# An attention-and-gate block on one core: keys in column tiles, norms on GpSimd, loads by use, level maxima

## The chip, the cores and the metric

The kernel runs on one core of a Trainium2 chip. The metric is the time of one execution on the device in microseconds (us). The core has TensorE (PE; its weight loads are shown apart as PEld), VectorE (DVE), ScalarE (ACT), GpSimd (POOL) and SyncE (SP), which here issues nearly all transfers.

## What is computed

x is 2048 rows of 512. It is normalised by rows; from the result come a 32-head attention with one shared key and value head of 16 columns, and a two-layer network with Mish between (1792 hidden). The output is x + attention * silu(network):

```python
xn = _layernorm(x, axis=-1)
q = (xn @ wq).reshape(B, S, 32, 16).transpose(0, 2, 1, 3)
k, v = xn @ wk, xn @ wv
p = softmax(einsum("bhqd,bkd->bhqk", q, k) * 16 ** -0.5)
s = einsum("bhqk,bkd->bhqd", p, v).transpose(0, 2, 1, 3).reshape(B, S, 512) @ wo
h = xn @ w1 + b1
g = silu((h * tanh(softplus(h))) @ w2)
return x + s * g
```

## The kernel before, in words

The program is written out by a Python planner: which instruction follows which on an engine is fixed when the program is built; on the chip each engine takes its own list in order and waits for semaphores.

**Blocks.** Rows are taken in four blocks of 512 (C). The attention runs in 32 units (NU), each of four heads of one block: unit v is block v // 8. A unit takes 16 steps of 128 keys, 512 steps (NS) in all.

**A step of the main loop** (the loop at L1483 with waves at L637) has on TensorE: four score products e (e_one, L1028; keys by queries on 64 rows), four products m for a *later* unit's row maxima (m_one, L1048; queries by keys, on 64 or 48 rows), and, for step s - 2, the value products pv (L1113, four column tiles of 32). ScalarE takes the exponentials of e, VectorE the maximum of each m (L1064). The maxima lead by LEAD = 20 steps. The array is used as two halves of 64 rows: one half's matmuls run beside the other's. e of a step stand on one half (a = 1 - s % 2); a chunk of dense-layer products (xps) is cut in half by rows (Mm.half), and runs on the one half in one step and on the other in the next, so each chunk takes two steps.

**Which maxima stand where.** em (L1490) calls m_sides (L1072) with the half of the e: n of the step's maxima go to that half, among the e (EM), the rest to the half of the dense products, where waves issues them behind the last of these. tot is 4, or 5 and then 3 for an odd chunk; MLAG = 4 bounds how far one side may lead; m_next counts the maxima issued of each side.

**Dense work.** Groups of products wait in queue and qqueue: queries (12 products), first layer m1 (12), second layer m2 in thirds of 5, 5 and 4 hidden tiles (15, 15 and 12 products) for four row tiles, and the output projection wo (12). begin (L501) takes the next that is ready, chunk_size (L634) cuts it into equal chunks of at most XMAX = 8: 12 as 6 + 6, 15 as 8 + 7. Weights come by load (L456) in the order of the tags (wq, ws, wb, wx) through two raw buffers and are split by split (L414) into a high and a low part; later blocks load the stored split.

**The lead-in** is planned as tasks with assumed durations, priorities and earliest times (L1382 to L1470): for each block statistics (stats, on VectorE, block 3's on ScalarE), norms (norm_a, norm_b, norm_c), scaling of x (x_scale), transposes (x_transpose), copies (x_copy), then keys and values in one product of 128 columns (k_proj, L315): wkf holds the key weights seven times (columns 0 to 47 and 64 to 111 are used for ks) and the value weights at the end. k_high (ScalarE) and k_low (VectorE) write high and low parts of the keys in place into ks; v_copy, v_transpose and v_out make the values. Query rows reach their places in qt by SP transfers (dmas, L723: twelve for each of the first two units). Between these stand the first maxima, 40 for each side, in pairs; after 34 of each side c_rows (L1082) reduces the first unit's and moves them by eight transfers, and the main loop starts when they land.

Of the kernel before, what the change touches and what calls it, by code (L numbers as in the profile page):

```python
# [80 lines left out]
class Item:  # L81
    def __init__(self, tag, key, src):
        self.tag, self.key, self.src = tag, key, src
        self.raw = self.tile = None
        self.step = None
        self.users = 0


class Group:
# [35 lines left out]
def block_kernel(ctx: ExitStack, tc: tile.TileContext, x, wq, wk, wv, wo, w1, b1, w2, out):  # L125
# [127 lines left out]
    def norm_a(z):  # L253
        if z.start >= A_LO:
            dve.tensor_scalar(ve[:, z], mvs[:, z, 1], 1.0 / D, EPS, op0=ALU.mult, op1=ALU.add)
        else:
            dve.tensor_scalar(ve[:, z], mvs[:, z, 1], EPS, None, op0=ALU.add)
# [5 lines left out]
    def norm_c(z):  # L263
        r, h = rstd[:, z], hv[:, z]
        stt(h, ve[:, z], -0.5, r, ALU.mult, ALU.mult)
        mul(dve, h, h, r)
        stt(r, h, 1.5, r, ALU.add, ALU.mult)
        if z.start >= A_LO:
            mul(dve, nbias[:, z], nbias[:, z], r)
        else:  # L270
            stt(nbias[:, z], mvs[:, z, 0], -1.0, r, ALU.mult, ALU.mult)
# [43 lines left out]
    def k_proj(c, dts):  # L315
        if 0 in dts:
            kp_of[c] = ps_v.tile([P, C], F32, tag="v", name=f"kp{c}")
        for dt in dts:
            pe.matmul(kp_of[c], wkf[:, dt], xf_of[c][dt // 2][:, dt % 2], start=(dt == 0), stop=(dt == 3))  # L319

    KR = slice(0, 112)

    def k_high(c):
        act.activation(ks[KR, C * c:C * (c + 1)], kp_of[c][KR], AF.Identity, bias=kone[KR])

    def k_low(c):
        k = ks[KR, C * c:C * (c + 1)]
        stt(k, f(k), ksgn[KR, 0:1], kp_of[c][KR], ALU.mult, ALU.add)
        kready[c] = now[0] + 0.85

    def v_copy(c):
        vt_of[c] = sb.tile([P, C], F32, tag=f"y{(2, 3, 1, 2)[c]}", name=f"vt{c}", bufs=1)[0:32]
        act.activation(vt_of[c], kp_of[c][96:128], AF.Copy)

    def v_transpose(c):
        vp = vp_of[c] = ps_v.tile([P, 4, 32], F32, tag="v", name=f"vp{c}")
        for tt in range(4):
            pe.transpose(vp[:, tt], vt_of[c][:, P * tt:P * (tt + 1)], ident[0:32, 0:32])

    def v_out(c):  # L340
        dve.tensor_copy(vaug[:, 4 * c:4 * c + 4, 0:DH], vp_of[c][:, :, 16:32])
# [139 lines left out]

    def pump():
        for tag in items:
            while arrived(tag):
                split(tag)
            load(tag)
# [9 lines left out]
    def prepare():  # L496
        for n in range(min(2 if step[0] < NS - LEAD else 8, len(queue))):
            if queue[n].pre and queue[n].pre():
                queue[n].pre = None

    def begin():  # L501
        prepare()
        if qqueue and is_ready(qqueue[0]):
            g = qqueue.popleft()
        elif queue and is_ready(queue[0]):
            g = queue.popleft()
        else:
# [12 lines left out]
        return True  # L520
# [35 lines left out]
    def next_group(z):  # L556

        if cur["g"] is not None:
            lanes[z] = [cur["g"], cur["n"], cur["ps"], None]
            cur["g"] = None  # L560
            return
# [72 lines left out]
    def chunk_size(n):  # L634
        return -(-n // -(-n // XMAX)) if n else 0

    def waves(h, em, new):  # L637
# [6 lines left out]
        else:  # L644
            g = cur["g"]
            mms = cur["chunk"] or g.mms[cur["n"]:cur["n"] + chunk_size(len(g.mms) - cur["n"])]
# [57 lines left out]
    def q_group(c, b):  # L704
        it = item("wq", ("q", b), wq[:, P * b:P * (b + 1)].rearrange("(t p) n -> p t n", p=P))

        def post(ps):
# [12 lines left out]
            for k in range(2):  # L720
                v = 8 * c + 2 * b + k

                def dmas(v=v, k=k, parts=((0, 0), (0, 1), (1, 0), (1, 1))):  # L723
                    q = qt_of[v] = qts[v % 3]
                    for p, a in parts:
                        o = 64 * a
                        r = 64 * k + 16 * (2 * p + a)
                        for d, src in ((o, qh), (o + 16, qh), (o + 32, ql)):
                            sp_at(0.63)
                            sp.dma_start(f(q[d:d + 16, p]), f(src[r:r + 16]))  # L730
                if first:
                    lead["qdma"](lambda ps, dmas=dmas: dmas(parts=[(p, a) for p in ps for a in range(2)]))
# [286 lines left out]
    queue.extend(wo_groups(NC - 1))  # L1019

# [51 lines left out]
    def m_sides(h, k, second):  # L1072
# [6 lines left out]
        n = max(min((k + tot - 4) // 2 if k % 2 else k // 2, hi), lo)  # L1079
# [143 lines left out]

    def when(t):
# [3 lines left out]
        if k <= step[0] and busy[0] + E0 < t + 0.5 and not plan["POOL"]:  # L1228
# [16 lines left out]
    def put_off(g, ps):  # L1245
# [4 lines left out]
        t = task("ACT", 0.69, fn, at=now[0] + lead.get("late", 0.35))  # L1250
# [4 lines left out]
    def q_low(fn):  # L1255
        lead["qlow"] = task("DVE", 0.69, fn, at=T["ACT"] + 0.7)

    def q_dma(fn):
# [3 lines left out]
        def move(p):  # L1262
            fn(ps=(p,))
            qready[v] = (qready[v] or ()) + (now[0] + 6 * 0.63 + 2.0,)
        for p in range(2):
            task("SP", 6 * 0.63, lambda p=p: move(p), [lead["qlow"]], prio=1 + p + 2 * v)
# [25 lines left out]
    st = [task("DVE", 0.83, lambda t=t: stats(t), at=max(xat[t], 15.5 if t > 3 else 0), prio=(0, 1.6, 2.2, 2.8)[t // 4]) for t in range(A_LO)]  # L1292
# [5 lines left out]
    for c0, c1 in ((0, 1), (1, 2), (2, 3), (3, 4)):  # L1298
        z = slice(4 * c0, 4 * c1)
        na = task("DVE", 0.2, lambda z=z: norm_a(z), st[z], prio=c0 and 1)  # L1300
        nb = task("ACT", 0.45, lambda z=z: norm_b(z), [na])
        nrm = task("DVE", 0.8, lambda z=z: norm_c(z), [nb], prio=2 * c0 and 1)
        for c in range(c0, c1):
            xs, scs = [], []
            for t in range(4 * c, 4 * c + 4):
                sc = task(*(("ACT", 0.72), ("DVE", 0.4))[c == 0 and t % 2], lambda t=t: x_scale(t), [nrm])
# [28 lines left out]
            else:  # L1335
# [3 lines left out]
                task("SP", 1.0, keep_x, xs)  # L1339
# [3 lines left out]
            kus = 0.9  # L1343
# [4 lines left out]
            kh = task("ACT", 0.59, lambda c=c: k_high(c), [kp])  # L1348
            kl = task("DVE", 0.68, lambda c=c: k_low(c), [kh])

            vc = task("ACT", 0.59, lambda c=c: v_copy(c), [kp])
# [33 lines left out]
    while True:  # L1385
# [25 lines left out]
        for tag in items:  # L1411
            load(tag)
# [31 lines left out]
        elif k == "J":  # L1444
            tag = next((g for g in ("wq", "ws", "wb") if (g == "wq" or s > 19.0) and arrived(g) and busy[0] + E0 < s + 0.5), None)
# [4 lines left out]
            else:  # L1450
                gap[0] = 0
                if not plan["POOL"]:
# [111 lines left out]
```

## Time and profile before

| | |
|---|---|
| median of 3 runs | 1581.02 us (1580.65 to 1581.16) |
| the profiled execution | 1580.51 us, its span 1578.7 us |
| granted clock of TensorE | 1.00 |
| busy, PE / DVE / ACT / POOL | 99 / 85 / 83 / 40% of the span |
| first score product e | 78.5 us after the span's start |
| DMA | 124.31 MB, mean 79 GB/s |

In rows of the profile, a group or a line of the timeline names the source line, the engine, the operation, the tile written and the tiles read, and their shapes; "x8" is a count of merged instructions. Lines of the timeline begin with the start and the duration in us; in groups the numbers are busy us, mean ns of one, and the engine's idle time before them with what released it. A window line gives start:end, its length, then busy time (and count) of PE, PEld, DVE, ACT and POOL, the granted clock, the share of the DMA engines and GB/s. SPq is SP's queue. A busy TensorE is not TensorE at its peak.

### The profile page before, as it was taken

The page shows a single profiled execution, that of the slowest core. Times are in us where ns is not written, and L with a number is a line of the kernel's source. Part 1 is how long each engine was busy: PE and PEld are TensorE (multiplying, and loading weights), DVE is VectorE, ACT ScalarE, POOL GpSimd, SP SyncE. Part 2 cuts the span into 40 slices and gives each one's busy share as a digit, 9 for nine tenths or more (in the row PEclk, how much of TensorE's full clock was granted, in tenths as well). Part 3 has the DMA queues.
Part 4 walks back from the last instruction along what each step waited for, and adds up shares of the span by engine and source line. Part 5 has one row for each costly group of instructions (what it writes and reads, how often), then busy time and mean ns, then how long its engine had stood idle before and what let it go on. Part 6 is the DMA issues. An engine that isn't in the chain of part 4 may idle for free.

```text
span 1578.7 us, 31652 instructions
## 1 busy us (share of the span) xinstructions
PE 1566.1 (99%) x11717; PEld 842.6 (53%) x11717; DVE 1341.9 (85%) x2341; ACT 1306.6 (83%) x2515; POOL 626.4 (40%) x641
## 2 busy tenths in 40 slices
PE   9999999999999999999999999999999999999998
PEld 5455555555555555555555555555555555555554
DVE  8998888889889888888898988888889998888832
ACT  7488798798998778978988787897898878789886
POOL 3476266274474104613525131362252414225412
PEclk9999999999999999999999999999999999999999
DMA  6233221132321304222122312220332213032011
GB/s 195 94 117 112 65 100 43 55 125 84 124 91 47 103 15 151 58 71 67 39 79 71 109 61 62 81 71 16 124 98 85 69 54 102 18 111 58 15 58 51
DMA packets 74666, 124.31 MB, mean 79 GB/s; under 512 B 21520, under 2 KB 35344, under 8 KB 74512
## 3 DMA queue, kind: packets, MB, share of 16 engines
q1 hardware_dynamic: 74512, 122.29, 25.1%
q8 instruction: 93, 1.52, 0.4%
q14 instruction: 61, 0.50, 0.1%
HBM read 74.78 MB, written 26.21 MB: 64 GB/s over the span
## 4 chain that ended last, share of the span: by engine, by line
PE 96%; DVE 2%; ACT 1%; DMA 0%; SPq 0%; issue 0%; POOL 0%; ACTq 0%; DVEq 0%
PE xps L118 44%; PE pv L1122 32%; PE e L1039 8%; PE m L1060 8%; DVE mb L1064 2%; PE kp L319 1%; PE xps L114 0%; ACT pt L1041 0%; PE xp L287 0%; PE late L118 0%; DMA xin<-in_dram 0%; PE late L1039 0%; PE wop L114 0%; DVE xt L162 0%; SPq L224 0%
## 5 line engine op out<-in xcount | busy, mean ns | idle before, releaser
L1064 DVE TENSOR_REDUCE mb<-m 128x1 f32<-128x512 f32 x2048 | 1274.0, 683 | 175.0 <-PE m L1060 153.4
L1041 ACT ACTIVATE pt<-e 128x512 f32<-128x512 f32 x2018 | 1061.9, 603 | 219.3 <-PE e L1039 210.6
L1060 PE MATMUL m<-ks,qt 48*128 48x512 f32 (+1 forms) x2048 | 830.5, 421 | 1.7 <-DVE mb L1064 0.8
L1039 PE MATMUL e<-qt,ks 64*128 64x512 f32 x2018 | 741.2, 401 | 0.5 <-ACT pt L1041 0.3
L1122 PE MATMUL pv<-pt,vaug 128*32 128x512 f32 x4096 | 543.0, 604 | 0.0
L1060 PEld LDWEIGHTS m<-ks,qt 48*128 48x128 f32 (+1 forms) x2048 | 372.5, 185 | 63.0 <-DVE mb L1064 25.3
L1039 PEld LDWEIGHTS e<-qt,ks 64*128 64x128 f32 x2018 | 373.3, 186 | 18.5 <-ACT pt L1041 6.7
L118 PE MATMUL xps<-wbs,act 64*128 64x512 f32 x1248 | 338.1, 407 | 0.1
L118 PEld LDWEIGHTS xps<-wbs,act 64*128 64x128 f32 x1248 | 217.6, 185 | 172.2 <-ACT pt L1041 100.7
L118 PE MATMUL xps<-xt,ws 64*128 64x512 f32 x1104 | 306.0, 410 | 0.1
L118 PEld LDWEIGHTS xps<-xt,ws 64*128 64x128 f32 x1104 | 190.2, 185 | 183.2 <-ACT pt L1041 116.5
L172 POOL TENSOR_SCALAR t<-t 128x512 f32<-128x512 f32 x56 | 34.4, 614 | 329.3 <-ACT t L784 328.9
L1122 PEld LDWEIGHTS pv<-pt,vaug 128*32 128x32 f32 x4096 | 81.9, 108 | 136.9 <-issue 128.8
L162 POOL TENSOR_TENSOR hb<-hb,t 128x512 f32<-128x512 f32 x56 | 72.3, 1290 | 64.2 <-ACT t L797 44.1
L118 PE MATMUL xps<-xt,wq 64*128 64x512 f32 x336 | 93.2, 410 | 0.0
L118 PEld LDWEIGHTS xps<-xt,wq 64*128 64x128 f32 x336 | 57.9, 185 | 55.5 <-ACT pt L1041 35.2
L118 PE MATMUL xps<-wbs,ot_all 64*128 64x512 f32 x288 | 79.5, 408 | 0.0
L118 PEld LDWEIGHTS xps<-wbs,ot_all 64*128 64x128 f32 x288 | 49.5, 184 | 46.4 <-ACT pt L1041 30.2
L162 POOL TENSOR_TENSOR hb<-hb,u 128x512 f32<-128x512 f32 x56 | 72.3, 1291 | 4.4
L162 POOL TENSOR_TENSOR u<-u,t 128x512 f32<-128x512 f32 x56 | 71.8, 1282 | 4.7
L162 POOL TENSOR_TENSOR act<-hb,act 128x512 fp32r<-128x512 f32 x55 | 70.8, 1287 | 4.6
L162 POOL TENSOR_TENSOR oc<-oc,sc 128x512 f32<-128x512 f32 (+1 forms) x16 | 20.6, 1288 | 116.5 <-ACT sc L1150 72.0
(146 smaller groups left out, 945.6 us busy)
## 6 DMA issues: line engine op xcount, KB each, us to landing
wbs<-w SPq DMA_DIRECT2D x36, 512.0 KB
ws<-w SPq DMA_DIRECT2D x35, 512.0 KB
qt<-qh SPq DMA_DIRECT2D x256, 32.0 KB
wq<-wq SPq DMA_DIRECT2D x14, 512.0 KB
w<-wbs SPq DMA_DIRECT2D x14, 512.0 KB
wbs<-wo SPq DMA_DIRECT2D x12, 512.0 KB
rawws<-in_dram SPq DMA_DIRECT2D x21, 256.0 KB
rawwb<-in_dram SPq DMA_DIRECT2D x20, 256.0 KB
```

The source lines that it names most:

```text
L118: i = self.pe.matmul(ps, self.lhs()[o], self.rhs()[o], start=(self.k == 0 and self.halves == 0), stop=(self.k == self.tot - 1 and self.hal ...
L162: eng.tensor_tensor(out=o, in0=a, in1=b, op=op)
L172: pool.tensor_scalar(o, o, lim, 0.0, op0=ALU.min, op1=ALU.max)
L319: pe.matmul(kp_of[c], wkf[:, dt], xf_of[c][dt // 2][:, dt % 2], start=(dt == 0), stop=(dt == 3))
L1039: pe.matmul(e, ks[o:o + 64, P * k:P * (k + 1)], q[o:o + 64, p], start=True, stop=True)
L1041: r = act.activation(pt, e, AF.Exp, scale=0.25)
L1060: pe.matmul(m, q[o, p, P * t:P * (t + 1)], ks[o, C * kb:C * (kb + 1)], start=True, stop=True)
L1064: r = dve.reduce_max(out=mb_of[v][:, kb, z:z + 1], in_=m, axis=AX.X)
L1122: pe.matmul(o[32 * j:32 * j + 32], vaug[:, k], pt, start=(k == 0), stop=(k == 15))
```

## The change

Keys and values of blocks 1 to 3 are projected with 64 columns of weights in two column tiles, each for half of the block's rows (256), so that the product stands as 128 partitions by 256. High and low parts are made there, in vt, and four transfers for a block place them in ks (k_rows); values are transposed from the same layout. Norms of blocks 1 to 3 and their scaling of x go to GpSimd. The statistics of blocks 2 and 3 are planned from 19.6 us. The first unit's first query rows go partly by ScalarE's queue. Loads are taken in the order in which groups use them. A group of 15 products may be cut in fives (most) when there are steps to spare before the first output projection. m_sides moves one maximum to the other half when the sides are not level. Some waits of the planner for GpSimd look only at tasks that are due.

```diff
+        self.most = XMAX
...
     def norm_c(z):
-        r, h = rstd[:, z], hv[:, z]
+        r, h, b = rstd[:, z], hv[:, z], nbias[:, z]
+        if z.start:
+            charge(1.1)
+            pool.tensor_tensor(out=h, in0=ve[:, z], in1=r, op=ALU.mult)
+            pool.tensor_tensor(out=h, in0=h, in1=r, op=ALU.mult)
+            pool.tensor_scalar(h, h, -0.5, 1.5, op0=ALU.mult, op1=ALU.add)
+            pool.tensor_tensor(out=r, in0=h, in1=r, op=ALU.mult)
+            if z.start < A_LO:
+                pool.tensor_scalar(b, mvs[:, z, 0], -1.0, 0.0, op0=ALU.mult, op1=ALU.add)
+            pool.tensor_tensor(out=b, in0=b, in1=r, op=ALU.mult)
+            return
...
     def x_scale(t):
         x_ = xin[divmod(t, 4)]
-        if t < 4 and t % 2:
+        if t > 3:
+            charge(0.7)
+            pool.tensor_scalar(x_, x_, rstd[:, t:t + 1], nbias[:, t:t + 1], op0=ALU.mult, op1=ALU.add)
+        elif t % 2:
...
+            for h in range(2):
+                pe.matmul(kp_of[c][HALF * h:HALF * (h + 1), 0:KW], wkf[:, dt, HALF:P], x_[:, KW * h:KW * (h + 1)],
+                          start=(dt == 0), stop=(dt == 3))
...
     def k_low(c):
+        if c:
+            st = vt_of[c][:, KW:C]
+            stt(st.bitcast(F32R), st, ksgn[:, 0:1], kp_of[c][:, 0:KW], ALU.mult, ALU.add)
+            return
...
+    def k_rows(c):
+        for a in range(2):
+            for h in range(2):
+                z = C * c + KW * h
+                sp.dma_start(f(ks[HALF * a:HALF * a + 48, z:z + KW]), vt_of[c][HALF * h:HALF * h + 48, KW:C])
+        kready[c] = now[0] + 4 * 0.63 + 2.1
...
+    def by_use():
+        return sorted(items, key=lambda g: items[g][todo[g][1]].use if todo[g][1] < len(items[g]) else 10 ** 6)
+
+    def load_next():
+        order = [g for g in by_use() if todo[g][1] < len(items[g])]
+        for tag in order:
+            for g in order:
+                it, n = items[g][todo[g][1]] if todo[g][1] < len(items[g]) else None, todo[g][1]
+                if g != tag and it and it.use + 3 < items[tag][todo[tag][1]].use and not kept.get(it.key) and (
+                        before(g, n) is None or not before(g, n).users):
+                    break
+            else:
+                load(tag)
...
+    def spare_steps():
+
+        n = next((n for n, g in enumerate(queue) if g.wo is not None), None)
+        if n is None or queue[n].wo:
+            return 0
+        due = 16 * 8 * (queue[n].wo + 1) + 9
+        return due - step[0] - 11 - 4 * (1 + n + sum(32 * (16 - k) - LEAD - 20 < due for k in range(1, len(qqueue) + 1)))
...
+        if len(g.mms) == 15 and spare_steps() > 1:
+            g.most = 5
...
-    def chunk_size(n):
-        return -(-n // -(-n // XMAX)) if n else 0
+    def chunk_size(n, most):
+        return -(-n // -(-n // most)) if n else 0
...
+    for n, g in enumerate(queue):
+        for i in g.items:
+            i.use = i.use or n
+    for n, i in enumerate(items["wq"]):
+        i.use = 8 * n - 7
...
-        n = max(min((k + tot - 4) // 2 if k % 2 else k // 2, hi), lo)
+        n = (k + tot - 4) // 2 if k % 2 else k // 2
+        off = ahead + 2 * n - tot - 2 * h
+        if k and abs(off) > 1:
+            n -= 1 if off > 0 else -1
+        n = max(min(n, hi), lo)
         return n, tot - n
...
+        if not v:
+            fn(parts=[(0, 1)], which=(0, 1), eng=act)
         for p in range(2):
-            task("SP", 6 * 0.63, lambda p=p: move(p), [lead["qlow"]], prio=1 + p + 2 * v)
+            n = 6 if v or p else 3
+            task("SP", n * 0.63, lambda p=p, n=n: move(p, n), [lead["qlow"]], prio=1 + p + 2 * v)
...
-    st = [task("DVE", 0.83, lambda t=t: stats(t), at=max(xat[t], 15.5 if t > 3 else 0), prio=(0, 1.6, 2.2, 2.8)[t // 4]) for t in range(A_LO)]
+    st = [task("DVE", 0.83, lambda t=t: stats(t), at=max(xat[t], (0, 15.5, 19.6, 19.6)[t // 4]), prio=(0, 1.6, 2.2, 2.8)[t // 4]) for t in range(A_LO)]
...
+            if c:
+                kr = task("SP", 4 * 0.63, lambda c=c: k_rows(c), [kl], prio=-4)
+                task("SP", 1.0, keep_x, [kr, *xs])
```

More of the change, by code (lines that the diff above doesn't have):

```diff
@@ L1222, in block_kernel, with pool_due @@
     now = [0.0]
+    def pool_due():
+        return any(all(d.end is not None for d in k.deps) for k in plan["POOL"])
     def when(t):
@@ L1227, in when @@
         k = min(timed, default=1)
-        if k <= step[0] and busy[0] + E0 < t + 0.5 and not plan["POOL"]:
+        if k <= step[0] and busy[0] + E0 < t + 0.5 and not pool_due():
             timed[k].pop(0)()
@@ L1249, in fn @@
             g.done = step[0]
-        t = task("ACT", 0.69, fn, at=now[0] + lead.get("late", 0.35))
+        t = task("ACT", 1.95 if "late" in lead else 0.69, fn, at=now[0] + lead.get("late", 0.35))
         waiting.append(t)
@@ L1255, in q_low @@
     def q_low(fn):
-        lead["qlow"] = task("DVE", 0.69, fn, at=T["ACT"] + 0.7)
+        lead["qlow"] = task("DVE", 0.69, fn, at=T["ACT"] + 0.7, prio=-4)
     def q_dma(fn):
```

82 lines of the change are left out of this document (52 added, 30 removed).

## The prediction

> **What bounds the kernel now.** I read the busy shares and the chain of waits on the page first, then four stretches, then single steps of the main loop on TensorE.
>
> ```profile
> PE 1566.1 (99%) x11717; PEld 842.6 (53%) x11717; DVE 1341.9 (85%) x2341; ACT 1306.6 (83%) x2515; POOL 626.4 (40%) x641
> ...
> PE 96%; DVE 2%; ACT 1%; DMA 0%; SPq 0%; issue 0%; POOL 0%; ACTq 0%; DVEq 0%
> ```
>
> ```profile
> 0.00:78.50 78.50, 73.71 (x292) 41.28 (x294) 70.54 (x148) 48.45 (x107) 34.45 (x44) 1.00 0.48 146
> 78.50:1506.00 1427.50, 1425.69 (x10942) 764.82 (x10940) 1253.96 (x2125) 1204.23 (x2303) 579.94 (x586) 1.00 0.25 76
> ```
>
> TensorE is busy throughout, but in the first 78.5 us part of that is warming and waiting for VectorE; the clock is 1.00 in both stretches. The lead-in is 5% of the span. The other 1427.5 us are some 490 equal steps, so an edit that touches each step's order weighs more than one in the lead-in. Two neighbouring steps, from one pv burst to the next:
>
> ```profile
> 1455.37 1.06 PE L1122 MATMUL pv<-pt,vaug 128*32 128x512 f32 x8
> ...
> 1457.87 0.39 PE L1060 MATMUL m<-ks,qt 48*128 48x512 f32 x1
> 1457.88 0.42 PE L1039 MATMUL e<-qt,ks 64*128 64x512 f32 x1
> 1458.23 1.07 PE L1122 MATMUL pv<-pt,vaug 128*32 128x512 f32 x8
> ...
> 1460.96 0.40 PE L1039 MATMUL e<-qt,ks 64*128 64x512 f32 x1
> 1460.97 0.40 PE L118 MATMUL xps<-wbs,act 64*128 64x512 f32 x1
> 1461.29 1.07 PE L1122 MATMUL pv<-pt,vaug 128*32 128x512 f32 x8
> ```
>
> The first carries six half products (xps), four e and four m: 14 half-array matmuls, seven to each row half, so seven slots; it lasts 1458.23 - 1455.37 = 2.86. The second carries eight, four and four: 16, eight to each half, and lasts 3.06. So a step's length is the count of slots of the **fuller row half**, and one more slot costs 0.2. A step whose halves are uneven stands in this trace too:
>
> ```profile
> 535.34 1.06 PE L1122 MATMUL pv<-pt,vaug 128*32 128x512 f32 x8
> ...
> 538.05 1.06 PE L1122 MATMUL pv<-pt,vaug 128*32 128x512 f32 x8
> 539.04 0.50 PE L118 MATMUL xps<-wbs,act 64*128 64x512 f32 x1
> 539.05 0.49 PE L1060 MATMUL m<-ks,qt 48*128 48x512 f32 x1
> ...
> 539.62 0.39 PE L1060 MATMUL m<-ks,qt 48*128 48x512 f32 x1
> ...
> 540.55 0.63 PE L118 MATMUL xps<-wbs,act 64*128 64x512 f32 x2
> 541.02 0.63 PE L1060 MATMUL m<-ks,qt 48*128 48x512 f32 x2
> 541.58 0.64 PE L1122 MATMUL pv<-pt,vaug 128*32 128x512 f32 x4
> ```
>
> It has the same eight xps, four e and four m, but only two m run beside the products and two run behind them on the products' own half: ten slots against six. It lasts 541.58 - 538.05 = 3.53, which is 0.47 more than the even step: 0.235 for each m left over. The step before it (535.34 to 538.05) has no product and lasts 2.71.
>
> **The levelled maxima.** This is the part that decides. m_sides gives n of a step's maxima to the half that holds the four e, and the rest to the half that holds the products. For eight products the old rule takes n = 4 of 4: sides 8 and 8. The new rule computes off = ahead + 2n - tot - 2h and takes one from n when off is above 1. The count of maxima done is equal on both sides when the loop begins (the lead-in issues them in pairs), call the lead of side 0 over side 1 A = 0. A chunk starts on an even step, with h = 1: off = 0 + 8 - 4 - 2 = 2, so n = 3 and A becomes -2. The next step has h = 0: off = -2 + 8 - 4 = 2, so n = 3 again and A returns to 0. Both steps of every eight-product chunk now have 4 + 3 = 7 matmuls on one half and 8 + 1 = 9 on the other: one slot more. With six products off is 0 in both steps (n = 3, seven and seven as before). With seven, off is 1 and then 0, nothing changes either. A can only be even where a chunk starts, since a pair of steps always takes eight maxima, and for an even A the eight-product chunk is never left alone: from A = 2 or -2 one of its steps is trimmed, and A is 0 after it. An odd start (after one empty step) gives the same with A = -2. So the rule makes this one chunk uneven for good.
>
> How many such steps there are follows from one row of the main loop's groups (line, operation, shapes, count):
>
> ```profile
> L118 PE MATMUL xps<-wbs,act 64*128 64x512 f32 x1218 | 329.9, 407 | 0.1
> ```
>
> These are the halves of the second dense layer. Twelve groups of 12 products (last third, three blocks) make 12 x 24 = 288; the remaining 930 are 31 groups of 15, which are cut 8 + 7, and each eight takes two steps: 62 steps. The limit of five (g.most) takes some away: spare_steps counts 126 - s - 4(1 + groups ahead of the first output projection + q groups due). At the first such group, s is about 16 with 22 groups and 4 q groups ahead: 126 - 16 - 108 = 2, just above 1; the next sees 0. It returns 0 for every later block. So about one group (none to three) is cut 5 + 5 + 5, and 60 (56 to 62) steps stay. 60 x 0.235 = **+14.1** (56 x 0.20 = 11.2 to 62 x 0.24 = 14.9). No other engine hides it: in the main stretch VectorE is busy 1254 and ScalarE 1204 of 1427.5 us.
>
> The group cut in fives gains about 0.8: four steps of 8, 8, 8 and 7 slots, 3 x 3.06 + 2.86 = 12.0, become three pairs of 7 and 6 slots, 3 x (2.86 + 2.71) = 16.7 with the empty step as the floor, and two of these six stood empty before (5.4). And the uneven step at 538 loses one of its two extra slots, 0.24: together **-1.0** (0 to -3). Loading in order of use may remove the empty steps (some three, 2.7 each), but what they take up is worth only its slots.
>
> **The lead-in.** From the first maximum to the last one needed (68 of 80) VectorE sets the pace; the window and its groups, shortened to those touched:
>
> ```profile
> 24.40:72.70 48.30, 47.09 (x185) 23.44 (x183) 46.06 (x83) 30.72 (x70) 19.89 (x19) 1.00 0.36 115
> ```
>
> ```profile
> L1064 DVE TENSOR_REDUCE mb<-m 128x1 f32<-128x512 f32 x68 | 42.2, 683 | 2.7 <-PE m L1060 2.4
> L237 DVE SCALAR_TENSOR_TENSOR ks<-ks,ksgn,kp 112x512 fp32r<-112x512 f32 x3 | 2.2, 736 | 0.0
> L237 DVE SCALAR_TENSOR_TENSOR hv<-ve,rstd 128x4 f32<-128x4 f32 x2 | 1.2, 578 | 0.0
> ...
> L162 DVE TENSOR_TENSOR hv<-hv,rstd 128x4 f32<-128x4 f32 x2 | 0.3, 162 | 0.1
> L237 DVE SCALAR_TENSOR_TENSOR rstd<-hv,rstd 128x4 f32<-128x4 f32 x2 | 0.3, 162 | 0.1
> ...
> L255 DVE TENSOR_SCALAR ve<-mvs 128x4 f32<-128x4 f32 x1 | 0.2, 190 | 0.0
> L237 DVE SCALAR_TENSOR_TENSOR nbias<-mvs,rstd 128x4 f32<-128x4 f32 x1 | 0.2, 161 | 0.0
> L162 DVE TENSOR_TENSOR nbias<-nbias,rstd 128x4 f32<-128x4 f32 x1 | 0.2, 161 | 0.0
> ```
>
> Norms leave VectorE: 1.2 + 0.3 + 0.3 + 0.2 + 0.2 + 0.2 = -2.4. The three low halves of the keys shrink from 512 to 256 columns: between no gain (0.74 each) and half (0.37), I take 0.42, near the half since the row count stays: 3 x 0.32 = -0.95. VectorE's idle time there is 48.30 - 46.06 = 2.24, mostly for m behind key matmuls; two column tiles side by side halve those, or run one after the other and save nothing: -1.0 (0 to -2.2). The start:
>
> ```profile
> 20.38 0.69 ACT L324 ACTIVATE ks<-kp,kone 112x512 fp32r<-112x512 f32 x1 [0.83 <-PE kp L319]
> ...
> 20.59 0.66 DVE L230 BATCH_NORM_STATS2 st<-xin 128x6 f32<-128x512 f32 x1
> ...
> 21.39 0.13 DVE L237 SCALAR_TENSOR_TENSOR hv<-ve,rstd 128x4 f32<-128x4 f32 x1
> ...
> 22.07 0.75 DVE L237 SCALAR_TENSOR_TENSOR ks<-ks,ksgn,kp 112x512 fp32r<-112x512 f32 x1
> ```
>
> The first keys' high part is done at 21.07, the low part starts at 22.07 behind a statistic and a norm; these go ahead of it no more, -1.0 (0 to -2.5: the first q rows, two of whose six transfers move to ScalarE's queue, must land by then as well). Against it, block 2's statistics now begin no earlier than 19.6: I put two of four, 0.66 + 0.18 each, behind the first maximum: +1.7 (0 to 3.4). Sum of the lead-in: **-3.6** (-8 to +3).
>
> What moves elsewhere is covered or not as follows. The 12 scalings cost GpSimd 12 x 0.61 = 7.4 us, its norms 18 small operations of about 0.18:
>
> ```profile
> L172 POOL TENSOR_SCALAR t<-t 128x512 f32<-128x512 f32 x56 | 34.4, 614 | 329.3 <-ACT t L784 328.9
> ...
> 6.85 1.29 POOL L350 COPY wkf<-wkv 128x64 f32<-128x64 f32 x7 [1.08 <-DMA wkv<-in_dram]
> ```
>
> that is 0.9 a block (0.3 to 4), and GpSimd is busy 34 of 78.5 us, so both lie beside VectorE's maxima, unless a weight split stands in front. The Trainium skill's GPSIMD Engine Reference (4.1, engine selection) speaks against this part: two-input elementwise work is about twice as slow there and belongs on VectorE. By it a block's four products and sums would take about 1.3 us, an estimate from that page's ratio and VectorE's 0.16 rows, and the sum would be the same to within 1 us, since VectorE is the fuller engine.
>
> Each later block's keys gain four SP transfers. Their price:
>
> ```profile
> 73.77 5.34 SPq L1109 DMA_DIRECT2D qt<-cr  x8
> ...
> 78.50 0.18 PEld L1039 LDWEIGHTS e<-qt,ks 64*128 64x128 f32 x1
> ```
>
> Eight issues take 5.34, the first four end at 76.44, the e that needs them starts 2.1 later. So keys come 4 x 0.6 + 2.1 = 4.5 later than their low part, against ScalarE's 4 scalings (2.9) and half the key matmuls saved; the maxima of the block before (16 x 0.6 = 10 us) cover that. Behind these transfers in SP's order stand weight loads, and the stored xt, whose users come after the loop has begun. The two issues on ScalarE's queue (0.6 each) stand ahead of its next statistics, not of the keys.
>
> **Sum:** 1578.7 + 14.1 - 1.0 - 3.6 = 1588.2 of span. The profiled execution took 1580.51, 1.8 more than its span, and the median of the runs is 0.5 above it: **1590.5**.
>
> **Rivals.** (1) *The ninth slot is free*, because a lone matmul on one half overlaps the pv burst, or the uneven step at 538 was long for another reason (ScalarE released an e late there). Then only the lead-in counts: 1581.0 - 4.6 = 1576.4, faster. Against it: in that step the products' half never paused, and the two m are its last two slots. It decides if eight-product steps stay at 3.06. (2) *Keys late on SP's queue*: a key transfer stands behind a load that waits for a buffer which GpSimd frees, and GpSimd has the scalings in front. Such waits exist now, by the table of who waited for whom on SP's queue (total, times, longest):
>
> ```profile
> SPq L474 <- POOL ws L162: 8.3, 1, 8.3
> ```
>
> With about 3 us a block on two blocks the lead-in turns to +3 and the time is 1597. Against it: the key transfers have the highest priority. (3) *The change levels less than it says or cuts more groups in fives*: with all eight eligible groups in fives, 46 steps stay (+10.8), 0.8 x 8 comes back, and with the best lead-in the time is 1581 + 10.8 - 6.4 - 4 = 1581, no difference. Against it: spare is 2, not 16.
>
> **Numbers.** Forecast 0.66 (its own range 1586 to 1594), rival 1 0.18, rival 2 0.09, rival 3 0.07 (half of it above 1584). A measurement of this kernel tells 0.2%, 3.2 us, from no change. Faster: 0.18. Same: 0.05. Slower: 0.66 + 0.09 + 0.02 = 0.77. The range reaches down into rival 1 and up into rival 2: 1577 to 1596.
>
> **What would show it.** In the changed profile: steps with eight products last about 3.29, with one m alone behind the last product; steps with six stay at 2.85; the first e starts near 75; VectorE's groups show no norms behind block 0 and low parts near 0.4. The forecast is wrong if eight-product steps stay at 3.06, or if hardly any are left, or if the first e starts after 78.5.

## The result and the profile after

The changed kernel takes 1603.86 us (median of 5 runs, 1603.56 to 1605.81), the kernel before 1581.04 beside it: a ratio of 1.0141, with an interval of 1.0124 to 1.0157. It is 23 us slower: the direction is the forecast's, the size is 13 more than its 1590.5 and outside its range (1577 to 1596).

The busy shares and the chain of waits on the page of the changed kernel:

```profile
PE 1583.0 (99%) x11725; PEld 854.9 (53%) x11725; DVE 1342.0 (84%) x2324; ACT 1296.7 (81%) x2501; POOL 637.8 (40%) x671
...
PE 94%; DVE 3%; ACT 1%; POOL 0%; DMA 0%; issue 0%; SPq 0%; ACTq 0%; POOLq 0%; DVEq 0%
```

The work of VectorE is what it was (1342.0 against 1341.9), TensorE still looks full, and the span is 1601.8. To see where 23.1 us of span went, take it by stretches: the first maximum to the last one needed, then the main loop from the first e on.

```profile
24.30:81.25 56.95, 50.93 (x223) 27.79 (x221) 43.46 (x75) 22.95 (x61) 31.72 (x43) 0.88 0.36 112
...
87.40:1534.00 1446.60, 1444.33 (x10954) 777.46 (x10951) 1261.05 (x2130) 1208.60 (x2308) 578.62 (x583) 1.00 0.24 76
```

The first stretch was 48.30 long and is 56.95. VectorE does less in it (43.46 us, before 46.06) and idles 13.5 (before 2.24). The first e starts at 87.4 instead of 78.6: **+8.8**. The main loop, from the first e to where the maxima end, took 1430.8 and takes 1446.8: **+16.0**. What remains behind it took 69.3 and takes 67.55: **-1.75**.

VectorE's groups in the first stretch say what it waits for:

```profile
L1141 DVE TENSOR_REDUCE mb<-m 128x1 f32<-128x512 f32 x68 | 42.1, 683 | 14.7 <-PE m L1137 14.7
L239 DVE SCALAR_TENSOR_TENSOR vt<-vt,ksgn,kp 128x256 fp32r<-128x256 f32 x3 | 1.4, 473 | 0.0
```

The norms are gone from VectorE, and a low part takes 0.47 where 0.42 was forecast. The idle time in front of the maxima was 2.7 in the same group before, 2.4 of it behind m; it is 14.7 now, all of it behind m (1.2 of it ahead of the window's start).

In the main loop, a step of the second layer with eight products, on TensorE (start, duration, operation):

```profile
1396.72 1.07 PE L1203 MATMUL pv<-pt,vaug 128*32 128x512 f32 x8
...
1398.99 0.40 PE L120 MATMUL xps<-wbs,act 64*128 64x512 f32 x1
1399.01 0.40 PE L1116 MATMUL e<-qt,ks 64*128 64x512 f32 x1
1399.23 0.40 PE L120 MATMUL xps<-wbs,act 64*128 64x512 f32 x1
1399.24 0.40 PE L1116 MATMUL e<-qt,ks 64*128 64x512 f32 x1
1399.46 0.39 PE L120 MATMUL xps<-wbs,act 64*128 64x512 f32 x1
1399.70 0.39 PE L1137 MATMUL m<-ks,qt 48*128 48x512 f32 x1
1400.01 0.64 PE L1203 MATMUL pv<-pt,vaug 128*32 128x512 f32 x4
```

The last e of the step starts at 1399.24. Behind it one half stays empty, and the eighth product and a ninth matmul, the lone m, follow alone on the other. The step lasts 1400.01 - 1396.72 = 3.29, the forecast's number.

### The profile page after: what moved, and what is told of

Read it like the earlier page. It is cut to its first block, busy times and chain, and to the rows that moved or that the text cites. A ratio compares the mean times of both kernels' runs of the same rounds, so it can differ in the third digit from the quotient of the medians.

```text
span 1601.8 us, 31706 instructions
## 1 busy us (share of the span) xinstructions
PE 1583.0 (99%) x11725; PEld 854.9 (53%) x11725; DVE 1342.0 (84%) x2324; ACT 1296.7 (81%) x2501; POOL 637.8 (40%) x671
## 4 chain that ended last, share of the span: by engine, by line
PE 94%; DVE 3%; ACT 1%; POOL 0%; DMA 0%; issue 0%; SPq 0%; ACTq 0%; POOLq 0%; DVEq 0%
PE xps L120 46%; PE pv L1203 31%; PE m L1137 8%; PE e L1116 7%; DVE mb L1141 2%; PE xps L116 1%; ACT pt L1118 1%; PE late L120 0%; PE xp L300 0%; DMA xin<-in_dram 0%; POOL xin L287 0%; PE kp L337 0%; PE late L1116 0%; PE late L116 0%; PE wop L116 0%
## 5 line engine op out<-in xcount | busy, mean ns | idle before, releaser
L1203 PEld LDWEIGHTS pv<-pt,vaug 128*32 128x32 f32 x4096 | 81.9, 108 | 137.8 <-issue 129.2
L159 POOL TENSOR_SCALAR qh<-qf 128x512 fp32r<-128x512 f32 x15 | 9.3, 622 | 110.1 <-ACT qf L787 110.1
```

Of the source, the lines that this page charges most:

```text
L159: pool.tensor_scalar(o, i, 1.0, 0.0, op0=ALU.mult, op1=ALU.add)
L1203: pe.matmul(o[32 * j:32 * j + 32], vaug[:, k], pt, start=(k == 0), stop=(k == 15))
```

## The experiments

Four causes were weighed: the fuller row half (called S in what was expected), norms and scaling on GpSimd (G), keys in column tiles placed by transfers (K), and the order that the plan then makes of TensorE's work (O). Edits are against the changed kernel, unless the text says otherwise. "First e" is from one profiled execution, and a time that stands without a ratio, a range or a count of runs is that of a single execution. In the cuts of code, "..." marks lines left out.

**The sides alone, in the kernel before.**

```diff
-        n = max(min((k + tot - 4) // 2 if k % 2 else k // 2, hi), lo)
+        n = (k + tot - 4) // 2 if k % 2 else k // 2
+        off = ahead + 2 * n - tot - 2 * h
+        if k and abs(off) > 1:
+            n -= 1 if off > 0 else -1
+        n = max(min(n, hi), lo)
```

> The kernel before with the new rule for the maxima's sides and nothing else. Theory S (one slot): each of the 62 steps with eight products lasts about 3.29 instead of 3.06, the step at 538 about 3.3 instead of 3.53; the lead-in keeps its first e at 78.5; time 1581.0 + 62 x 0.235 = 1595.6. Rival (the main loop grew for another reason, the order of loads or the fives): eight-product steps stay near 3.06 and the time stays within 2 us of 1581.

1593.47 us, a ratio of 1.0082 (1.0067 to 1.0097), 13.0 more than before. The first e stays at 78.3. The 62 steps with eight products take 3.30 on the mean instead of 3.09: 62 x 0.21 = 13.0. These few lines give more than half of the loss, with nothing else changed.

**The sides undone, the rest of the change kept.**

```diff
-        off = ahead + 2 * n - tot - 2 * h
-        if k and abs(off) > 1:
-            n -= 1 if off > 0 else -1
```

> The changed kernel with the old rule for the maxima's sides. Theory S: eight-product steps return to 3.06, the main loop shortens by 60 x 0.235 = 14.1, the lead-in stays as in the changed kernel (first e at 87.4); time 1603.9 - 14.1 = 1589.8. Rival (the sides matter only together with the rest): the time stays above 1600.

A miss: 1612.73 us (1.0205, 1.0188 to 1.0222), slower than the changed kernel. The eights do return to 3.07 (median; the mean is 3.11), but seven steps where a unit begins last 5.0 to 5.6, and the step behind each, at a lowered clock (last section), 3.8 to 4.4: together some 25 us. One of the seven in the timeline (in brackets the wait before an instruction and what ended it):

```profile
321.72 0.20 DVE L1179 STREAM_TRANSPOSE cr<-mp 128x32 f32<-128x32 f32 x1
...
321.95 5.32 SPq L1187 DMA_DIRECT2D qt<-cr  x8
...
322.39 1.06 PE L1200 MATMUL pv<-pt,vaug 128*32 128x512 f32 x8
...
325.83 0.47 PE L1116 MATMUL e<-qt,ks 64*128 64x512 f32 x1 [1.71 <-DMA qt<-cr]
...
327.54 1.08 PE L1200 MATMUL pv<-pt,vaug 128*32 128x512 f32 x4
```

The maxima rows of the next unit are reduced at 321.72 and issued at 321.95; the e that reads them is due at 324.1 and waits until 325.83, and the step lasts 5.15. The table of waits of the main loop counts seven such waits of e, and two more where its weight load stood first:

```profile
PE e L1116 <- DMA qt<-cr: 11.7, 7, 1.7
...
PEld e L1116 <- DMA qt<-cr: 4.0, 2, 2.0
```

So in the changed schedule the rule has a use that the forecast did not see: without it the last maxima of some units come too late for their transfers.

**The sides levelled only in steps with fewer than eight products.**

```diff
-        if k and abs(off) > 1:
+        if 0 < k < 8 and abs(off) > 1:
```

> The changed kernel with the new side rule kept for chunks below eight products and left off for eights. Theory S: eights return to 3.06 (60 x 0.235 = 14.1 less). Theory W (the rule is there to have a unit's last maxima in time): no e waits for the transfers of the maxima, as it does seven times with the old rule throughout; together the main loop takes 1432 to 1434 us and the time is about 1590. Rival (eights need the levelling too): e waits for these transfers again and the time is above 1595.

1589.77 us. The first e is at 87.3 as before the edit, no e waits for a transfer of maxima, the eights take 3.08 and the main loop 1433.2 instead of 1446.8. **13.6 us of the change's loss is the ninth slot** (60 x 0.223 = 13.4 in the eights themselves), and it can be taken back without undoing the rule. The end of such a step in its timeline, with the sides at eight and eight:

```profile
1384.96 1.06 PE L1203 MATMUL pv<-pt,vaug 128*32 128x512 f32 x8
...
1387.46 0.40 PE L120 MATMUL xps<-wbs,act 64*128 64x512 f32 x1
1387.48 0.39 PE L1137 MATMUL m<-ks,qt 48*128 48x512 f32 x1
1387.70 0.39 PE L120 MATMUL xps<-wbs,act 64*128 64x512 f32 x1
1387.71 0.40 PE L1116 MATMUL e<-qt,ks 64*128 64x512 f32 x1
1388.04 0.64 PE L1203 MATMUL pv<-pt,vaug 128*32 128x512 f32 x4
```

**Norms and scaling back on VectorE and ScalarE.** norm_a, norm_c and x_scale as in the kernel before, and their tasks planned there.

> The changed kernel with norms and scaling of blocks 1 to 3 back on VectorE and ScalarE. Theory G (GpSimd's scalings come late, TensorE idles behind them, its granted clock falls, and the maxima wait for TensorE): the clock stays at 1.00 from 40 to 80 us, VectorE's idle time before maxima falls from 14.7 to below 5, the first e comes before 80 instead of 87.4, time about 1595. Theory K (the keys' four transfers make them late): first e still above 85, VectorE still idles above 10 us.

1610.88 us, the first e at 96.2. G falls as the cause: with this part undone the lead-in is longer still. How much of the 7 us is the order, which moved again, or the granted clock, which was 0.78 from 24.3 to 40 us, was not taken apart.

**Keys of blocks 1 to 3 in place again.** k_proj, k_high, k_low, v_copy, v_transpose and v_out take their old form for all blocks, and k_rows goes.

> The changed kernel with the keys of blocks 1 to 3 projected in one tile of 128 columns and written in place, as before; norms and scaling stay on GpSimd. Theory K: the first e comes before 80 and VectorE idles below 5 us before maxima. Theory G: the gaps behind GpSimd stay, the clock still falls below 0.9 between 40 and 70 us, first e above 83.

1593.18 us, the first e at 78.2 (78.6 in the kernel before), VectorE's idle time behind m 4.6 in place of 14.7. The whole loss of the lead-in hangs on this one part.

**More warming, so that the clock holds.** In lead-in windows of 5 us the changed kernel shows TensorE slowed (behind the comma stand the busy times of the five engines, with counts in brackets, and then the granted clock):

```profile
45.00:50.00 5.00, 4.27 (x18) 2.61 (x18) 2.67 (x5) 2.16 (x7) 4.18 (x5) 0.67 0.81 274
50.00:55.00 5.00, 5.00 (x24) 2.36 (x22) 4.12 (x7) 1.51 (x5) 1.26 (x1) 0.64 0.25 65
55.00:60.00 5.00, 3.83 (x19) 1.72 (x17) 5.00 (x10) 1.05 (x3) 1.29 (x1) 1.00 0.20 54
60.00:65.00 5.00, 4.13 (x10) 2.26 (x10) 3.64 (x7) 1.97 (x4) 3.18 (x4) 0.54 0.38 112
```

Before, it was 1.00 throughout. The edit puts warming matmuls ahead of each later tile's transposes:

```diff
         xp_of[t] = ps.tile([P, NDT, P], F32, tag=tag, name=f"xp{t}")
+        if c:
+            keep_warm(4)
         for dt in range(NDT):
```

> The changed kernel with four dummy matmuls (128x512) on TensorE ahead of each transpose group of blocks 1 to 3, 48 in all. Theory C (TensorE's idle gaps lower its granted clock, and the slow matmuls make the lead-in long): the clock stays near 1.00 from 40 to 70 us and the first e comes before 83 instead of 87.4, although 48 matmuls of 0.23 us are added. Theory O (the order: keys come late and TensorE has long chunks of dense products in front of the maxima): the clock rises but the first e stays at 86 to 92.

1607.26 us, the first e at 91.0. The clock is 1.00 up to 60 us, and VectorE idles 18.9. But it does not weigh the clock by itself: 55 warming matmuls in place of 7 occupy TensorE for 16.7 us in place of 2.6.

**The plan told that keys are ready early; the low part first; block 3 alone; eight small transfers.** Four edits of the numbers by which the plan is made:

```diff
-        kready[c] = now[0] + 4 * 0.63 + 2.1
+        kready[c] = now[0] + 0.85
```

> The changed kernel, but the planner takes the keys as ready 0.85 us after the low part is planned, as before, and not after 4 x 0.63 + 2.1 us; the waits on the chip stay. Theory O (the allowance, that is the planned order, puts dense products ahead of the maxima): first e before 83. Theory L (the transfers' real latency): TensorE waits for the key transfers by name, VectorE idles more than 14.7 us, first e at 87 or later.

1601.38 us, the first e at 84.2. Neither theory came out whole: the first e is 3.3 earlier but not before 83, and m now waits for the key transfers by name, 4.1 us in all, which it never does in the changed kernel.

```diff
-            kl = task("DVE", 0.4 if c else 0.68, lambda c=c: k_low(c), [kh])
+            kl = task("DVE", 0.4 if c else 0.68, lambda c=c: k_low(c), [kh], prio=-4 if c else 0)
```

> The changed kernel with the keys' low part of blocks 1 to 3 ahead of planned maxima on VectorE (priority -4). Theory V (the low part stands behind maxima on VectorE for up to 2.8 us, and the transfers start late for that): transfers start within 1 us of the high part's end, first e 3 to 6 us earlier, 82 to 84. Rival (another link of the keys' chain comes last): first e within 1 us of 87.4 or later.

1602.40 us, the first e at 86.2. This edit moved nothing: on VectorE, ScalarE and GpSimd every instruction stands in the order of the changed kernel, and block 3's low part still starts 3.2 us after its high part, as at 56.15 and 59.35 there:

```profile
56.22 0.39 ACT L346 ACTIVATE vt<-kp 128x256 fp32r<-128x256 f32 x1 [4.13 <-PE kp L337]
...
59.41 0.47 DVE L239 SCALAR_TENSOR_TENSOR vt<-vt,ksgn,kp 128x256 fp32r<-128x256 f32 x1
```

So theory V stays untested, and the run is one more execution of the changed kernel.

```diff
-        kready[c] = now[0] + 4 * 0.63 + 2.1
+        kready[c] = now[0] + (0.85 if c == 3 else 4 * 0.63 + 2.1)
```

> The changed kernel; only for block 3 the planner takes the keys as ready 0.85 us after the low part is planned. Blocks 1 and 2 are planned as in the changed kernel, so what comes before block 3's keys stays where it is. Theory O (the 7.3 us between the landing of block 3's keys, 64.3, and their first maximum, 71.6, are dense products put ahead by the plan): that maximum follows the landing within 1.5 us, and the first e comes 4 to 7 us earlier, at 80.5 to 83.5. Theory L (only the transfers' latency counts): first e within 2 us of 87.4.

1601.34 us and the first e at 87.2, which by the expectation speaks for theory L. But that sets it beside a profile of another clock. The edit moved nothing ahead of block 3: VectorE's instructions stand in the same order through the whole lead-in, and TensorE's up to the last dense products before block 3's maxima. Yet block 2's first maximum came at 58.2 instead of 54.6, with a granted clock of 0.67 from 24.3 to 40 us instead of 1.00. The second profile of the changed kernel (last section) had 0.67 there as well; in it block 2's first maximum is at 58.8, and the first e at 90.4. Block 3's first maximum with the edit:

```profile
70.96 5.47 DVE L1141 TENSOR_REDUCE mb<-m 128x1 f32<-128x512 f32 x9 [1.23 <-PE m L1137]
```

and in that second profile, without it:

```profile
74.57 1.89 DVE L1141 TENSOR_REDUCE mb<-m 128x1 f32<-128x512 f32 x3 [3.77 <-PE m L1137]
```

At a similar clock the edit brings this maximum 3.6 us forward and the first e 3.2. That is nearly all that the same number gives for the three blocks together (3.3).

```diff
-                sp.dma_start(f(ks[HALF * a:HALF * a + 48, z:z + KW]), vt_of[c][HALF * h:HALF * h + 48, KW:C])
-        kready[c] = now[0] + 4 * 0.63 + 2.1
+                for y in range(2):
+                    w = P * y
+                    sp.dma_start(f(ks[HALF * a:HALF * a + 48, z + w:z + w + P]), vt_of[c][HALF * h:HALF * h + 48, KW + w:KW + w + P])
+        kready[c] = now[0] + 8 * 0.63 + 2.1
...
-                kr = task("SP", 4 * 0.63, lambda c=c: k_rows(c), [kl], prio=-4)
+                kr = task("SP", 8 * 0.63, lambda c=c: k_rows(c), [kl], prio=-4)
```

> The changed kernel with each of the four key transfers of a block split in two (eight of 128 columns; the planner's allowance grows with it). If a block's keys are late by the issue time of its transfers, 0.6 each, they land 2.4 us later for each of the three blocks, and the first e moves from 87.4 to between 90 and 95. If the transfers are hidden, it stays within 1 us.

A miss: 1602.26 us, the first e at 85.2, earlier with twice the issues. Here the plan did order the work otherwise from about 40 us on, with 72 full-array dense products ahead of the first e instead of 60. A dose test fails where the number also redraws the order.

**Keys in place, sides levelled below eight.** The two repairs together, and then with GpSimd's part undone as well.

> The changed kernel without its two costs: keys of blocks 1 to 3 in place as before, and the new side rule left off for chunks of eight. The first e should come at 78.2 as without the key transfers, the main loop take 1443.9 - 62 x 0.235 = 1429.4, the tail 69.3: span 1576.9, time 1578.7, 0.1% below the kernel before. If the other parts (GpSimd, loads in order of use) give nothing, it is 1580.5.

1582.78 us (12 runs, 1579.27 to 1584.25), a ratio of 1.0004 (0.9993 to 1.0016): no difference from the kernel before, to within -1 to +2.5 us. Its main loop takes 1430.9, as the kernel before's 1430.8. So without these two parts, what remains of the change neither loses nor wins more than that. The groups in fives are not in what remains: with keys in place and the plan told 0.85 us, the trace has no step with five products and 62 with eight.

> As the run before it, and norms and scaling also back on VectorE and ScalarE. If GpSimd's part saves lead-in time by itself, the first e comes 1 to 3 us after 78.2; if it gives nothing without the transfers, within 0.5 us of 78.2.

1584.88 us, the first e at 81.9 against 80.5. One execution, 0.6 above the highest of the twelve, with a clock of 0.78 from 24.3 to 40 us where the other had 1.00: it doesn't tell whether GpSimd's part saves anything.

**Lateness or order: the four cells.** Keys in place or by transfers, each with the plan told 0.85 or 4.6 us (4 x 0.63 + 2.1), in the same session. The new cell:

```diff
     k = ks[KR, C * c:C * (c + 1)]
     stt(k, f(k), ksgn[KR, 0:1], kp_of[c][KR], ALU.mult, ALU.add)
-    kready[c] = now[0] + 0.85
+    kready[c] = now[0] + (4 * 0.63 + 2.1 if c else 0.85)
```

> Keys of blocks 1 to 3 are again projected and split in place, without transfers, but the plan is told that they can be read as late as in the changed kernel (4 x 0.63 + 2.1 us after the low part instead of 0.85). If the longer lead-in comes from the order that the plan makes of that lateness (it puts dense products ahead of the maxima on TensorE), the first e comes near 84 to 87 and the time is near 1600 although no key is late on the chip. If it comes from the lateness of the transferred keys themselves, the first e stays at 78 to 80.5 and the time near 1593.

> Keys by transfers, and the plan told that they can be read 0.85 us after the low part. One look gave 1601.4 with the first e at 84.2. If only lateness counts, the time is that of the changed kernel, 1603.6; if only the order counts, that of the kernel with keys in place, 1593. Between them, as at the first look: both count.

> Keys of blocks 1 to 3 projected and split in place, and the plan told 0.85 us. One look gave 1593.2 with the first e at 78.2; the same lead-in in another kernel had it at 80.5. Expected 1593 to 1596, a spread of some 2 us between executions.

> The changed kernel beside the three others on the same chip: 1603.6, first e at 87.

| keys | plan told | median of 4 runs, us | ratio and interval | first e | full-array dense products in the lead-in |
|---|---|---|---|---|---|
| in place | 0.85 | 1595.41 (1592.84 to 1595.84) | 1.0088 (1.0073 to 1.0103) | 80.6, earlier run 78.2 | 42 |
| in place | 4.6 | 1596.64 (1596.41 to 1598.57) | 1.0103 (1.0086 to 1.0120) | 81.3 | 51 |
| transfers | 0.85 | 1601.37 (1601.06 to 1604.12) | 1.0133 (1.0118 to 1.0148) | 87.0, earlier run 84.2 | 45 |
| transfers | 4.6 | 1604.92 (1603.52 to 1606.38) | 1.0152 (1.0137 to 1.0167) | 90.4, earlier run 87.4 | 60 |

The new cell, in place with 4.6, comes out between its two expectations. Down a pair with the same plan number, the transfers cost 6.0 and 8.3 us, with intervals apart. Within a pair the plan's number costs 1.2 and 3.6, with intervals that overlap. The medians mix executions of different granted clock. The four profiles that had 1.00 from 24.3 to 40 us can be set against each other, though they are from different sessions: in the order of the table their first e is at 78.2, 81.3, 84.2 and 87.4. There the transfers cost 6.0 and 6.1, the plan's number 3.2 and 3.3, and the two together 9.2. After 40 us the clock stays at 1.00 in the two with keys in place, and falls to 0.54 in some windows of 5 us in the two with transfers.

The cells do not part lateness from order altogether: at the same number the plan with transfers still has more dense products ahead of the first e, 45 to 42 and 60 to 51. The products that the order brings forward can be counted in TensorE's groups from 20 us to the first e. With keys by transfers and 0.85 (the third row):

```profile
L116 PE MATMUL xps<-xt,ws 128*128 128x512 f32 x24 | 9.8, 524 | 0.0
...
L116 PE MATMUL xps<-xt,wq 128*128 128x512 f32 x12 | 6.6, 683 | 0.0
...
L116 PE MATMUL xps<-xt,early 128*128 128x512 f32 x9 | 2.6, 418 | 0.4 <-ACT hb L848 0.4
```

In the changed kernel (the first of its two profiles) the same three are 24, 12 and, in the last, 24:

```profile
L116 PE MATMUL xps<-xt,early 128*128 128x512 f32 x24 | 7.7, 430 | 0.7 <-ACT hb L848 0.7
L116 PE MATMUL xps<-xt,ws 128*128 128x512 f32 x24 | 7.4, 424 | 0.7 <-ACT qf L787 0.7
...
L116 PE MATMUL xps<-xt,wq 128*128 128x512 f32 x12 | 5.6, 606 | 1.9 <-ACT hb L848 1.9
```

Fifteen products more are 7.7 - 2.6 = 5.1 us of TensorE ahead of the first e. Between profiles of a similar clock the first e moves by 3.3, and the stretch behind the main loop pays back 1.75 (69.3 to 67.55). Their count alone does not set the first e: the kernel before has 51 and starts at 78.6, the one with eight transfers 72 and starts at 85.2. With transfers and 0.85 the maxima's products do reach the transfers too early, in the table of waits:

```profile
PE m L1137 <- DMA ks<-vt: 2.4, 3, 1.3
...
PEld m L1137 <- DMA ks<-vt: 1.6, 1, 1.6
```

These are up to 4.0 of the 6.0 that this cell loses to the one in place (4.1 in the earlier run). In the changed kernel no m waits for a key transfer.

## Why the prediction was wrong, by its steps

**The levelled maxima: right in mechanism and size.** +14.1 was forecast, and 13.6 measured when only the eights were set free. Sixty steps came, as counted, but the count is partly luck: two groups were cut in fives and not one, which leaves 58 (as in the run with block 3 alone told early), and the changed kernel has one chunk of eight more in its main loop, probably because the lead-in took more of the queue. Rival 1, a free ninth slot, falls, and so does rival 3, with two groups cut and not eight. (Of rival 3's 0.07, half above 1584 would be 0.035 and not the 0.02 that the sum of chances uses; nothing hangs on it.) What the step did not see is that the rule buys something: the run without it shows the late transfers of maxima.

**The lead-in: the step that failed.** The sum had -3.6 (-8 to +3), and +8.8 came. What it counted on VectorE held: 43.46 us of work instead of 46.06. The small terms of the start did not come: block 2's statistics end at 22.07, ahead of the first maximum (+1.7 forecast), and the first low part starts at 22.39 instead of 22.07 (-1.0 forecast). GpSimd's norms take 1.3 us a block; the forecast's own 18 operations of 0.18 make 1.1 and not 0.9. The lateness of the keys was sized about rightly, 4.5 us: in the trace the last transfer has landed 3.8 us after the low part's end for blocks 1 and 3, and 5.9 for block 2.

What failed is the sentence that "the maxima of the block before (16 x 0.6 = 10 us) cover that", by which the four transfers stand in the sum at nothing. Undoing this part alone takes the first e back from 87.4 to 78.2: it costs 9.2 us. The first maximum of blocks 0, 1, 2 and 3 of the keys started at 24.5, 39.7, 51.4 and 62.9 before, and at 24.3, 40.9, 54.6 and 71.6 after: each block loses more than the last. Block 3 in the timeline of the changed kernel:

```profile
56.15 0.38 ACT L346 ACTIVATE vt<-kp 128x256 fp32r<-128x256 f32 x1 [3.53 <-PE kp L337]
...
59.35 0.47 DVE L239 SCALAR_TENSOR_TENSOR vt<-vt,ksgn,kp 128x256 fp32r<-128x256 f32 x1
...
59.85 2.42 SPq L363 DMA_DIRECT2D ks<-vt  x4
...
60.87 1.65 PE L116 MATMUL xps<-xt,wq 128*128 128x512 f32 x3 [1.95 <-ACT hb L848]
...
63.28 1.29 DVE L1141 TENSOR_REDUCE mb<-m 128x1 f32<-128x512 f32 x2 [1.06 <-PE m L1137]
...
65.79 2.31 PE L116 MATMUL xps<-xt,wq 128*128 128x512 f32 x6
65.90 1.29 DVE L1141 TENSOR_REDUCE mb<-m 128x1 f32<-128x512 f32 x2 [1.20 <-PE m L1137]
...
68.79 1.66 PE L116 MATMUL xps<-xt,ws 128*128 128x512 f32 x6 [0.69 <-ACT qf L787]
...
71.61 1.89 DVE L1141 TENSOR_REDUCE mb<-m 128x1 f32<-128x512 f32 x3 [4.42 <-PE m L1137]
```

The last transfer is issued by 62.27 and has landed at 63.64; block 2's last maximum ends at 67.19; but m of block 3 runs only at 71.07. Between stand dense products that wait for ScalarE (1.95 and 0.69) and run slowed behind the longer of these waits (three in 1.65, where they take 0.96 with keys in place). So at this block it is not a transfer that VectorE waits for, but the products that the plan put ahead. With keys in place and 0.85, in the earlier run of that kernel, the same links read:

```profile
56.47 0.69 ACT L348 ACTIVATE ks<-kp,kone 112x512 fp32r<-112x512 f32 x1 [4.18 <-PE kp L334]
...
59.30 0.74 DVE L239 SCALAR_TENSOR_TENSOR ks<-ks,ksgn,kp 112x512 fp32r<-112x512 f32 x1
...
59.95 3.67 DVE L1141 TENSOR_REDUCE mb<-m 128x1 f32<-128x512 f32 x6
```

High part and low part end within 0.7 us of the other kernel's times, and VectorE goes on without a gap into block 3, whose first maximum is at 62.3. So the cover was thin: VectorE idled only 2.24 in 48.30 because a new block's keys were there as the last block's maxima ran out. The cells divide the loss: 6.0 to 8.3 for keys that arrive by transfers, 1.2 to 3.6 for the later time that the plan is told (6.0 and 3.2 of the first e at a similar clock). Of the first, up to 4.1 is shown as waiting for the transfers in the cell with 0.85. In the changed kernel there is no such wait, and how its 6 splits between the dense products put ahead and the slower clock stays open.

**Rival 2** came nearest, +3 for keys late on SP's queue, but not by its mechanism: in the changed kernel SP issues the transfers as the low part ends (59.82 to 59.85), with no load in front.

**The fives: mis-sized.** -1.0 was forecast, with one group cut and pairs of 2.86 and 2.71. Two groups were cut, and the six pairs take 3.24 and 2.85 on the mean. A pair's first step has five maxima beside five products; by slots it is seven against seven, as in the forecast, but the last two m come late, and the second step, with six slots, takes 2.83 to 2.87, no less than one with seven. With the eights set free the main loop is still 2.3 longer than before's (1433.2 to 1430.8), and with the 1.75 behind it +0.6 remains for fives, loads and the start of the loop. The fives are at most a part of the 2.3: 1.2 of it is there by the loop's tenth step, before the first chunk of five, and the kernel with transfers and 0.85, which cuts no group in fives, has a main loop 2.2 longer than the one with keys in place (1446.1 to 1443.9), with 2.1 of it in the first ten steps. That the late m wait for VectorE, which needs 5 x 0.62 for five maxima, was only argued.

The sum by what was measured: 13.6 + 8.8 + 0.6 = 23.0, of 23.1 in the span.

## What to carry to other kernels

Where a step is packed from two row halves, as here, its price was the fuller half: a rule that evens out a running count may unbalance every step it touches, and it should be held off where the step is full already. Before calling a latency covered, look at how much idle time its consumer had before: 2 us in 48 left no room here for 4.5 more per block. And an edit of one number of a plan may redraw all that follows it, a part of it, or nothing at all: compare the order of the instructions and the granted clock of the two executions before reading a difference of 3 us as the edit's. Cells of two by two, with repeats, told more than doses.

## What was not expected of the hardware

The same program shows different granted clocks in the lead-in, and with them different times. Two profiles of the changed kernel, from 24.3 to 40 us, the first with the first e at 87.4 (1603.56 us):

```profile
24.30:40.00 15.70, 14.66 (x85) 8.60 (x85) 12.99 (x23) 10.50 (x34) 7.34 (x15) 1.00 0.30 84
```

and the second at 90.4 (1606.38 us):

```profile
24.30:40.00 15.70, 15.70 (x67) 8.16 (x66) 12.05 (x21) 7.87 (x26) 7.47 (x14) 0.67 0.20 51
```

The kernel with keys in place shows the same pair: 1.00 with the first e at 78.2, 0.67 with 80.6. A clock of 0.67 over some 15 us of the lead-in thus goes with 2.4 to 3.0 us, which is most of the spread between the runs of these kernels. The kernel before was at 1.00 in every window of its profile, but two of its other executions have a mean clock of 0.995, where nearly all have 0.999 or 1.00, and take 1587.2 and 1587.4 us.

In the traces the drops stand behind pauses of TensorE. The clock is recorded there as either 1.00 or 0.50, and the windows show means. In the eighteen traces of this case, between 10 and 1540 us, each of the 22 pauses between matmuls of 1.5 us or more is followed, within 2.1 us of its end, by a clock of 0.50, for 3.4 us or longer; of the 13 pauses near 1.3 us, four are. The changed kernel has two of the long ones in its lead-in, 1.65 at 44.1 and 1.95 at 58.9 in the first profile; the kernel before has none above 0.7 there, the one with keys in place none above 1.31. The kernel with the sides undone shows it seven times in the main loop, by the waits of e above: the step with a pause of 1.71, and the one behind it:

```profile
322.39:327.54 5.15, 3.44 (x25) 1.61 (x23) 2.95 (x6) 2.23 (x6) 0.00 (x0) 0.97 0.03 6
327.54:331.79 4.25, 4.25 (x24) 2.01 (x23) 2.42 (x5) 2.57 (x6) 0.00 (x0) 0.64 0.72 243
```

The two profiles of the changed kernel part behind a pause of 1.0 and 1.2 us near 21.5 us, after which the clock fell in the second alone. The warming matmuls, which fill such pauses, kept the clock at 1.00 up to 60 us. That the pause is the cause was not tried by an edit that changes nothing else.
